# Other PSUM banks, and eleven fewer, for the zeros products at the head of a Nyströmformer attention and MLP kernel

## The chip, the core and the metric

The kernel runs on one core of one Trainium2 chip. The time is that of one execution on the device, in microseconds (us); lower is better. Before the change it is 262.47 us, the median of 3 runs (262.06 to 262.75).

## The reference

Inputs are q, k and v (batch 8, 8 heads, 576 positions, head size 64) and two weights. Per batch and head, with 32 landmarks, each the mean of 18 consecutive positions:

```python
q_lm = q.reshape(B, H, m, S // m, D).mean(axis=3)      # k_lm the same
A  = softmax(scale * q @ k_lm.T);  Bm = softmax(scale * q_lm @ k_lm.T);  C = softmax(scale * q_lm @ k.T)
Z  = Bm.T / (max column sum * max row sum + 1e-6)
for _ in range(6): Z = 2 * Z - Z @ Bm @ Z
x  = A @ Z @ C @ v                                     # heads side by side: 4608 rows of 512
out = square(maximum(x @ w_in, 0)) @ w_out             # w_in 512 x 2048, w_out 2048 x 512
```

The output is float32; on the chip the products are taken in bf16.

## The kernel before, in words

**What is computed where.** The work goes batch by batch. For one batch TensorE transposes q and k (L579) and sums them over each landmark's positions by products with a permutation matrix (L544, folded at L554); in the first two batches every one of these is a product on TensorE, with `perm` as the moving operand. From the sums come the landmark product Bm (L604 for batch 0, L607 for batch 1), on VectorE and ScalarE its softmax (L619 to L631) and transposed copy BTf (L633), and the start `st` of the iteration (L667, L669). Six products (L689 in batch 0) with an update each on VectorE (L704) give Z. Beside that run the scores of q against the landmarks (L873, then L884 to L912 on VectorE, POOL and ScalarE, up to the transposed matrix AT) and of the landmarks against k (L759; nmc, the negated maximum, L765; exponential L769; transposes L781; product with v L803). Z, that product and w_in are then multiplied into G (L853, L929), a 128 x 2 x 2048 matrix, so that the MLP's first layer is AT times G (L948), then relu and square (L965 to L975), then the second layer (L1020) and the stores.

**Overlap.** While the MLP of batch b runs, attention of batch b + 1 is worked in between. Only the head, batch 0, has nothing to run beside it.

**PSUM.** One tile `ps` holds the eight banks of 512 float32. Operations that need two neighbouring banks take the pairs 0-1 and 2-3; the others take single banks, 4 to 7. Which bank an operation takes is written in the order.

**The order.** `ORDER` (L40) is a list of integers, one operation each, in the order in which they are given to the engines. A positive code is 64 times the operation's number, plus 8 times the engine's (PE, ACT, DVE, POOL, SP), plus its bank. A negative code stands for zeros products:

```python
if code < 0:
    self.fill((-code) % 8, (-code) // 8)

def fill(bank, n):
    for _ in range(n):
        mm(ps[:, bank, 0:P], lhsT=zero[:], rhs=zero[:], start=True, stop=True)
```

So -479 is 59 products, 128 x 128 by 128 x 128, of a tile of zeros with itself, into bank 7. Nobody reads them. They keep TensorE at work where it would wait. They obey the same rules as other writers of a bank: the first of a set waits until what was in the bank has been read. Each engine works through its instructions strictly in order; semaphores between engines are set by a layer that tracks readers and writers of each tile region. `PACE` (below `ORDER`) adds waits by hand: an operation, mostly a load issued on POOL, then also waits for another operation.

**Loads.** q, k, v, w_in and w_out are loaded as float32 and cast to bf16 by DMAs issued on POOL; only the first half of k for batch 0 comes by SP in float32 and is cast by POOL and ScalarE (L304, L306). Stores go by SP.

**The head, in TensorE's order, with its sets of zeros products** (number and bank in the kernel before; the last column tells what stands behind and where it writes):

| set | products, bank | what follows it on TensorE |
|---|---|---|
| 1 | 59, bank 7 | first transposes of q (L579), bank 4; 9 sums over q (L544), bank 5 |
| 2 | 7, bank 7 | last transposes of k, bank 6 |
| 3 | 10, bank 6 | 18 sums over k (L544), bank 7; then 9 sums over q, 6 transposes, a fold, 6 transposes |
| 4 | 6, bank 4 | Bm (L604), bank 5 |
| 5 | 5, bank 4 | landmarks against k (L759), banks 0 and 1 |
| 6 | 1, bank 7 | first product of the iteration's start (L660), bank 5 |
| 7 | 9, bank 5 | first iteration (L689), bank 7 |
| 8 | 8, bank 4 | second iteration, bank 5 |
| 9 | 2, bank 7 | transposes of the exponentials (L781), bank 4 |
| 10 | 8, bank 7 | fourth iteration, bank 5 |
| 11 | 4, bank 7 | product with v (L803), banks 0 and 1 |
| 12 | 11, bank 7 | third part of G (L929), banks 0 and 1 |
| 13 | 5, bank 6 | fourth part of G, banks 2 and 3 |
| 14 to 16 | 1, 5 and 2, banks 7, 4, 4 | products of the MLP and of batch 1 |

Of the kernel before, what the change touches and what calls it, by code (L numbers as in the profile page):

```python
# [37 lines left out]
}  # L38

ORDER = [  # L40
    592, 32, 344, 280, 472, 720, -479, 2628, 2309, 160, 784, 408, 200, 88, -63, 2182, 2248, -86, 1607, 1664, 2696,
    1736, 2368, 2440, 2758, 1560, 1796, 1864, 2887, 2952, -52, 3013, 984, 2832, 6016, 3088, 3208, 3144, 1496, 2052,
    9734, 1927, 2120, 6096, 920, 2501, 2568, 1368, 1992, 6594, 1176, 3280, 3344, 856, 3408, 3536, 3464, -44, 4992,
    9476, 6672, 3600, 5072, 1048, 5128, 1112, -15, 3781, 3664, 3728, 3920, 3856, 9544, 4738, 4816, 4872, -77, 3975,
    4048, -68, 4101, 6160, -23, 5252, 4176, 5192, 6736, 4936, 1240, 4231, 4304, -71, 4357, 536, 4432, 5520, 5584,
    5320, 5383, 6232, 8772, 6280, 6352, 4485, 1432, 6808, 5448, -39, 5632, 4560, 4615, 9800, 6416, 9157, 6480, 5712,
    1304, 4688, 5890, 5760, 6856, 6928, 6992, 7064, 9606, 5968, 9216, 5832, 7168, 7240, 6544, 7362, 7312, 7432, 7120,
    8024, 7960, -95, 7552, 7696, 7496, 7624, 8455, 15170, 656, 15360, 8216, 8512, 15248, 15312, 9288, 9349, 9424,
    15432, 8584, 18328, 15554, 15744, 15632, 18456, 9680, 15496, 18392, 18264, 9031, 15816, 9096, 15896, 8645, -46,
    7746, 7824, 15936, 7880, 16008, 16088, 8848, 8902, 8976, -15, 16130, 16208, 8712, 8280, 15688, 16320, 16392, 9863,  # L50
    8088, 9936, 9992, 10056, -44, 13826, 13904, 16456, -20, 16512, 16584, 13250, 10128, 10192, 10256, 8152, 10312,
    10392, 10448, 10512, 16264, 13328, 10576, 13968, 22980, 23040, 16648, 23104, 16704, 16898, 16776, 16968, 8344,
# [1035 lines left out]
```

## Time and profile before

| | |
|---|---|
| median of 3 runs | 262.47 us |
| the profiled execution | 262.38 us |
| its span, first to last instruction | 260.7 us |
| mean granted TensorE clock | 0.998 |
| TensorE busy | 246.9 us, 95% |
| VectorE, ScalarE, POOL busy | 78%, 77%, 56% |
| moved by DMA | 28.60 MB |

All times inside the profile count from the start of the span; the execution's own time is 1.7 us longer. A timeline row gives start, duration, engine, line, operation, output and inputs, and, in brackets, how long the engine had stood idle and what ended that. Rows of one operation that follow each other are merged (x59). PE is TensorE's product, PEld its weight load. Products are pipelined, so that a merged row's duration ends later than the next row's start; the distance of two starts tells the pace. The row of a DMA issue gives the time that issuing took; the time from issue to landing stands in a view of its own.

### The profile page before, as it was taken

To read this page: it belongs to the slowest core of one execution; us is meant where nothing else is said; L and a number is where in the kernel's file an instruction comes from. 1 tells how busy PE (TensorE), PEld (TensorE's weight loads), DVE (VectorE), ACT (ScalarE), POOL (GpSimd) and SP (SyncE) were. 2 spreads that over 40 slices of the span, in tenths; PEclk is the share of its full clock that TensorE was granted. 3 is DMA by queue.
4 is the path that set the end of the run, shared out by engine and by line. 5 is a ranking of instruction groups with operands and counts; after the bars stand their busy time and mean duration, and the time that the engine had idled before them with its cause. 6 is when DMAs were issued, how large, how long until landed. Compare 5 with 4: busy or idle time off the path is not lost.

```text
span 260.7 us, 7783 instructions
## 1 busy us (share of the span) xinstructions
PE 246.9 (95%) x3012; PEld 147.2 (56%) x3051; DVE 202.1 (78%) x488; ACT 201.1 (77%) x417; POOL 146.4 (56%) x219
## 2 busy tenths in 40 slices
PE   8888889999999999999999999999999999999995
PEld 8866654545654555455645465555645556466552
DVE  0088789999998888979989889799998877934521
ACT  2586799997998898978997799866978877676410
POOL 7247675786777666765587456845464454531000
PEclk9999999999999999999999999999999999999999
DMA  6999999639901991097605981094503431013233
GB/s 161 209 178 167 189 208 208 112 51 164 213 14 24 195 214 51 2 153 176 119 4 87 212 174 31 22 191 105 97 11 48 103 73 43 0 44 70 62 93 112
DMA packets 20470, 28.60 MB, mean 110 GB/s; under 512 B 3280, under 2 KB 11728, under 8 KB 20432
## 3 DMA queue, kind: packets, MB, share of 16 engines
q0 software_dynamic: 13296, 18.06, 44.0%
q1 hardware_dynamic: 6848, 9.77, 13.0%
q8 instruction: 24, 0.39, 0.6%
q10 hardware_dynamic: 288, 0.26, 0.3%
q14 instruction: 14, 0.11, 0.1%
HBM read 36.70 MB, written 9.44 MB: 177 GB/s over the span
## 4 chain that ended last, share of the span: by engine, by line
PE 79%; DVE 8%; ACT 4%; issue 4%; POOL 4%; DVEq 0%; ACTq 0%
PE ps L1020 40%; PE ps L948 21%; PE ps L455 4%; PE ps L725 3%; PE ps L926 2%; POOL EA L901 2%; PE ps L544 2%; PE ps L781 2%; PE ps L803 2%; PE ps L694 1%; DVE SA L884 1%; ACT r L965 1%; POOL ks L512 1%; PE ps L579 1%; DVE nmc L765 1%
## 5 line engine op out<-in xcount | busy, mean ns | idle before, releaser
L1020 PE MATMUL ps<-w_out_bf,gs 128*128 128x512 bf16 (+1 forms) x553 | 139.1, 373 | 3.3 <-issue 2.2
L948 PE MATMUL ps<-AT,G 128*128 128x288 bf16 x512 | 79.0, 286 | 1.4 <-issue 0.8
L1020 PEld LDWEIGHTS <-gs 128*128 128x128 bf16 x592 | 53.5, 98 | 47.3 <-issue 8.1
L965 ACT ACTIVATE r<-ps 128x576 bf16<-128x576 f32 x108 | 68.1, 651 | 13.7 <-PE ps L948 11.6
L948 PEld LDWEIGHTS <-G 128*128 128x128 bf16 x512 | 48.7, 98 | 24.1 <-issue 1.1
L973 ACT ACTIVATE gs<-r 128x576 bf16<-128x576 bf16 x83 | 55.4, 682 | 4.1 <-DVE r L967 3.5
L975 POOL TENSOR_TENSOR gs<-r 128x576 bf16<-128x576 bf16 x22 | 25.2, 1151 | 18.3 <-DVE gs L975 9.4
L304 ACT CAST G<-ps 128x512 bf16<-128x512 f32 x47 | 24.8, 592 | 4.6 <-PE ps L926 3.1
L379 POOL DMA_DIRECT2D vraw<-in_v_dram x32 | 18.2, 570 | 16.9 <-DVE BTf L633 8.5
L304 ACT COPY o<-ps 128x512 f32<-128x512 f32 (+1 forms) x32 | 18.0, 569 | 11.6 <-PE ps L1020 11.6
L967 DVE TENSOR_SCALAR r<-ps 128x576 bf16<-128x576 f32 x20 | 15.1, 759 | 10.3 <-PE ps L948 7.9
L638 POOL TENSOR_TENSOR Pd<-st,ones_d 128x256 bf16<-128x256 bf16 x17 | 11.4, 671 | 12.2 <-DVE st L704 8.6
L746 ACT ACTIVATE EC<-ps,nmc 128x288 bf16<-128x288 f32 x24 | 11.7, 501 | 7.9 <-DVE nmc L739 6.3
L890 POOL TENSOR_TENSOR SA<-SA,mxA 128x576 f32<-128x576 f32 x12 | 13.9, 1161 | 6.8 <-DVE qs L512 3.8
L455 PE MATMUL ps<-zero 128*128 128x128 bf16 x143 | 13.4, 255 | 4.2 <-DVE zero L464 1.1
L901 POOL TENSOR_TENSOR EA<-EA,rA 128x576 bf16<-128x576 bf16 x13 | 15.0, 1158 | 2.5 <-DVE ks L512 1.0
L533 DVE STREAM_TRANSPOSE qT<-qraw 128x1152 bf16<-128x1152 bf16 x12 | 16.4, 1364 | 0.0
L533 DVE STREAM_TRANSPOSE kT<-kraw 128x1152 bf16<-128x1152 bf16 x12 | 16.1, 1348 | 0.0
L455 PEld LDWEIGHTS <-zero 128*128 128x128 bf16 x143 | 11.4, 118 | 5.5 <-issue 3.7
L704 DVE SCALAR_TENSOR_TENSOR st<-st,ps 128x128 bf16<-128x128 bf16 x40 | 11.1, 278 | 3.0 <-PE ps L689 1.1
L884 DVE STREAM_TRANSPOSE SA<-ps 128x576 f32<-128x576 f32 x16 | 12.0, 768 | 1.7 <-PE ps L725 1.1
L975 DVE TENSOR_TENSOR gs<-r 128x576 bf16<-128x576 bf16 x23 | 10.2, 450 | 3.5 <-ACT r L965 3.3
(146 smaller groups left out, 362.2 us busy)
## 6 DMA issues: line engine op xcount, KB each, us to landing
out_dram<-o SPq DMA_DIRECT2D x126, 64.0 KB, 3.2
qraw<-in_q_dram POOLq DMA_DIRECT2D x16, 288.0 KB, 5.6
vraw<-in_v_dram POOLq DMA_DIRECT2D x32, 144.0 KB, 5.6
kraw<-in_k_dram POOLq DMA_DIRECT2D x15, 288.0 KB, 6.5
w_in_bf<-in_moe_w_in_dram POOLq DMA_DIRECT2D x4, 512.0 KB, 7.8
w_out_bf<-in_moe_w_out_dram POOLq DMA_DIRECT2D x4, 512.0 KB, 9.3
out_dram<-o SPq DMA_DIRECT2D x3, 256.0 KB, 3.1
gs<-in_k_dram SPq DMA_DIRECT2D x2, 288.0 KB, 4.0
```

Of the source, the lines that this page charges most:

```text
L304: nc.scalar.copy(dst, src)
L379: nc.gpsimd.dma_start(vraws[z][p0:p0 + 32, :, :, :].rearrange("p g t d -> p g (t d)"), src[b].rearrange(order, i=2, t=SEG)[i, :, :, c * NJ ...
L455: mm(ps[:, bank, 0:P], lhsT=zero[:], rhs=zero[:], start=True, stop=True)
L533: add("hx", "DVE", lambda e, nm=nm, raw=raw, i=i: nc.vector.transpose(heads(nm)[:, i, :, :, :].rearrange("p t h r -> p (t h r)"), raw[:, i ...
L884: keep("a_t", add("a_t", "DVE", lambda e, sa=sa, i=i, part=part: nc.vector.transpose(part(SA).rearrange("p c j m -> p c (j m)") if quad el ...
L901: keep("a_mul", add("a_mul", "POOL DVE", lambda e, part=part, spread=spread: ENG[e].tensor_tensor(part(EA), part(EA), spread(part(rA)), AL ...
L948: mm(t[:, j, 0:HALF], lhsT=G[:, i, f * P:(f + 1) * P], rhs=AT[:, i, j * HALF:(j + 1) * HALF], start=(i == 0), stop=(i == 1))
L965: nc.scalar.activation(r.rearrange("p (j t) -> p j t", j=2), src, AF.Relu)
L967: nc.vector.tensor_scalar(out=r.rearrange("p (j t) -> p j t", j=2), in0=src, scalar1=0.0, scalar2=None, op0=ALU.max)
L973: nc.scalar.activation(dst, r[:], AF.Square)
L975: ENG[e].tensor_tensor(dst, r[:], r[:], ALU.mult)
L1020: mm(one(ok)[:, 0:hi - lo], lhsT=gs[:, f, x0:x0 + P], rhs=w_out_bf[:, f, lo:hi], start=(f == f0), stop=(f == f1 - 1))
```

## The change

Only `ORDER` changes, and in it only codes of zeros products. Everything else stands in the same order on every engine, and the operations keep their banks. Set 1 has 48 products instead of 59. Eleven sets write to another bank: sets 1, 2, 3, 4, 5, 10 and 11 to bank 0, set 6 to bank 5, set 7 to bank 7, set 8 to bank 5, set 9 to bank 4, set 13 to bank 2. So some now write the bank of the operation behind them, and some a bank of the pairs. The first product of a set then waits for the readers of its new bank.

```diff
 ORDER = [
-    592, 32, 344, 280, 472, 720, -479, 2628, 2309, 160, 784, 408, 200, 88, -63, 2182, 2248, -86, 1607, 1664, 2696,
-    1736, 2368, 2440, 2758, 1560, 1796, 1864, 2887, 2952, -52, 3013, 984, 2832, 6016, 3088, 3208, 3144, 1496, 2052,
-    9734, 1927, 2120, 6096, 920, 2501, 2568, 1368, 1992, 6594, 1176, 3280, 3344, 856, 3408, 3536, 3464, -44, 4992,
-    9476, 6672, 3600, 5072, 1048, 5128, 1112, -15, 3781, 3664, 3728, 3920, 3856, 9544, 4738, 4816, 4872, -77, 3975,
-    4048, -68, 4101, 6160, -23, 5252, 4176, 5192, 6736, 4936, 1240, 4231, 4304, -71, 4357, 536, 4432, 5520, 5584,
-    5320, 5383, 6232, 8772, 6280, 6352, 4485, 1432, 6808, 5448, -39, 5632, 4560, 4615, 9800, 6416, 9157, 6480, 5712,
+    592, 32, 344, 280, 472, 720, -384, 2628, 2309, 160, 784, 408, 200, 88, -56, 2182, 2248, -80, 1607, 1664, 2696,
+    1736, 2368, 2440, 2758, 1560, 1796, 1864, 2887, 2952, -48, 3013, 984, 2832, 6016, 3088, 3208, 3144, 1496, 2052,
+    9734, 1927, 2120, 6096, 920, 2501, 2568, 1368, 1992, 6594, 1176, 3280, 3344, 856, 3408, 3536, 3464, -40, 4992,
+    9476, 6672, 3600, 5072, 1048, 5128, 1112, -13, 3781, 3664, 3728, 3920, 3856, 9544, 4738, 4816, 4872, -79, 3975,
+    4048, -69, 4101, 6160, -20, 5252, 4176, 5192, 6736, 4936, 1240, 4231, 4304, -64, 4357, 536, 4432, 5520, 5584,
+    5320, 5383, 6232, 8772, 6280, 6352, 4485, 1432, 6808, 5448, -32, 5632, 4560, 4615, 9800, 6416, 9157, 6480, 5712,
...
-    15432, 8584, 18328, 15554, 15744, 15632, 18456, 9680, 15496, 18392, 18264, 9031, 15816, 9096, 15896, 8645, -46,
+    15432, 8584, 18328, 15554, 15744, 15632, 18456, 9680, 15496, 18392, 18264, 9031, 15816, 9096, 15896, 8645, -42,
```

## The prediction, made before the changed kernel had run

> **What bounds the kernel now.** I read the page's first part, then the busy times by stretch, then the timeline of the first 32 us, because every edit lies there. First the page: the span, each engine's busy time, and the group of zeros products.
>
> ```profile
> span 260.7 us, 7783 instructions
> ...
> PE 246.9 (95%) x3012; PEld 147.2 (56%) x3051; DVE 202.1 (78%) x488; ACT 201.1 (77%) x417; POOL 146.4 (56%) x219
> ...
> L455 PE MATMUL ps<-zero 128*128 128x128 bf16 x143 | 13.4, 255 | 4.2 <-DVE zero L464 1.1
> ```
>
> TensorE is the bound, and the 143 zeros products are only 13.4 us of its work; 4.2 us of its idle time end in front of one of them. Where that idle time lies, the stretches tell (length, busy time of PE, PEld, DVE, ACT, POOL, granted clock, DMA share, GB/s):
>
> ```profile
> 0.00:10.00 10.00, 8.05 (x92) 7.93 (x93) 0.61 (x4) 3.07 (x4) 6.60 (x16) 1.00 0.82 178
> 10.00:20.00 10.00, 8.83 (x190) 7.21 (x186) 6.43 (x19) 7.50 (x23) 3.58 (x8) 1.00 1.10 184
> 20.00:30.00 10.00, 8.69 (x221) 6.80 (x222) 8.35 (x21) 6.29 (x13) 6.70 (x8) 1.00 1.17 177
> 30.00:40.00 10.00, 8.86 (x101) 5.90 (x100) 8.16 (x19) 9.42 (x22) 7.84 (x12) 1.00 1.18 205
> ...
> 60.00:80.00 20.00, 19.63 (x257) 11.82 (x258) 19.56 (x50) 18.22 (x37) 14.37 (x20) 1.00 0.59 116
> ```
>
> From 60 us on TensorE is busy for 98% of the time, so what the head saves is kept to the end, if nothing but TensorE's order follows. In the first 40 us it is idle for 5.6 us, and there the sixteen DMA engines are full too (share above 1). So the head has two clocks: the chain of batch 0 through TensorE, ScalarE and VectorE, and the loads.
>
> **Step 1, eleven products fewer ahead of the first transposes.** The zeros products alone in the first stretch (length, PE busy and count, granted clock, DMA), then the timeline of the start, then the two loads' times to landing (last column):
>
> ```profile
> 1.06:6.80 5.74, 5.74 (x55) 1.00 0.83 194
> ```
>
> ```profile
> 1.06 6.22 PE L455 MATMUL ps<-zero 128*128 128x128 bf16 x59 [1.06 <-DVE zero L464]
> 1.34 0.74 POOL L374 DMA_DIRECT2D qraw<-in_q_dram  x1 [0.82 <-POOLq L1072]
> ...
> 2.07 0.55 POOL L374 DMA_DIRECT2D kraw<-in_k_dram  x1
> ...
> 6.37 0.67 ACT L304 CAST kraw<-gs 128x576 bf16<-128x576 f32 x1 [4.28 <-DMA gs<-in_k_dram]
> 7.12 0.50 PE L579 MATMUL ps<-perm,qraw 128*128 128x128 bf16 x6
> ...
> 7.96 0.55 PE L455 MATMUL ps<-zero 128*128 128x128 bf16 x7
> 8.35 0.50 PE L579 MATMUL ps<-perm,kraw 128*128 128x128 bf16 x6
> ...
> 8.88 0.80 ACT L304 COPY kT<-ps 128x768 bf16<-128x768 bf16 x1 [1.84 <-PE ps L579]
> 9.58 0.80 ACT L304 COPY qT<-ps 128x768 bf16<-128x768 bf16 x1
> 9.73 0.72 PE L455 MATMUL ps<-zero 128*128 128x128 bf16 x10 [0.89 <-ACT kT L304]
> ...
> 10.29 1.17 PE L544 MATMUL ps<-perm,kraw 128*128 128x128 bf16 x18
> ```
>
> ```profile
> qraw<-in_q_dram POOLq DMA_DIRECT2D x1, 288.0 KB, 4.7
> ...
> kraw<-in_k_dram POOLq DMA_DIRECT2D x1, 288.0 KB, 5.7
> ```
>
> A zeros product takes 5.74/55 = 0.104 us at the start; the fifteen q products take (7.96 - 7.12)/15 = 0.056 us each, and the ten zeros from 9.73 to 10.29 the same. TensorE starts at half speed, though the granted clock reads 1.00, and is fast from about 6.8 us. Eleven products fewer are 1.15 us at the slow pace, so the q transposes could start near 6.1 instead of 7.12. Their q lands at 1.34 + 4.7 = 6.04: no hindrance. But then 15 q products and 7 zeros follow, the first six or seven still slow (6.2 + 6 x 0.104 + 16 x 0.056 = 7.7), and the k transposes need k, landing at 2.07 + 5.7 = 7.8. With 0.15 us from landing to product they start at 7.95 instead of 8.35. **Gain 0.40**, not 1.15. In a run whose slow stretch ends earlier it is 0, with a later end up to 0.65.
>
> **Step 2, the ten zeros in front of the sums over k.** In the kernel before they go into bank 6 and wait until ScalarE has copied the k transposes out of it (8.88 + 0.80 = 9.68). The sums behind them need nothing of that copy: they go to bank 7, and the last of k that they read is cast at 6.37 + 0.67 = 7.04 (its other half has landed at 7.8). In bank 0 the zeros start behind the sixth transpose, 8.35 + 6 x 0.056 = 8.69 instead of 9.73: 1.05 us more, **1.45 in all**. ScalarE, next in the chain, has time: moved by 0.40 its second copy ends near 9.58 + 0.80 - 0.40 = 9.98, and the sums end near 10.0.
>
> **Step 3, six zeros in front of the first small product.**
>
> ```profile
> 12.24 0.50 PE L579 MATMUL ps<-perm,qraw 128*128 128x128 bf16 x6
> ...
> 12.44 0.37 ACT L304 CAST kdup<-ps 128x256 bf16<-128x256 f32 x1
> ...
> 12.87 0.49 PE L455 MATMUL ps<-zero 128*128 128x128 bf16 x6
> ...
> 13.29 0.23 PE L604 MATMUL ps<-kdup,qls 128*32 128x32 bf16 x8
> ```
>
> Zeros and product wait for the same cast (ends 12.81). Afterwards the zeros run while the cast does (12.58 to 12.91), and the product starts near 13.0 instead of 13.29: 0.29 more, **1.74**.
>
> **Step 4, the zeros ahead of the iterations.** The five and the one that come next lie beside a VectorE that is busy almost without a break (the row below, third engine); they are counted at nothing, and without that cover would be worth 0.1. Then the rows of the next two sets and of what waits for them:
>
> ```profile
> 14.80:18.50 3.70, 2.76 (x72) 1.96 (x69) 3.46 (x11) 2.87 (x7) 2.22 (x4) 1.00 1.19 186
> ```
>
> ```profile
> 17.64 0.21 DVE L667 TENSOR_TENSOR st<-BB,rc 128x64 bf16<-128x64 f32 x1
> ...
> 17.77 0.75 DVE L765 TENSOR_REDUCE nmc<-ps 128x1 f32<-128x576 f32 x1
> ...
> 18.36 0.24 PE L689 MATMUL ps<-st 32*32 32x64 bf16 x8
> ...
> 18.72 0.29 DVE L704 SCALAR_TENSOR_TENSOR st<-st,ps 128x128 bf16<-128x128 bf16 x1 [0.20 <-PE ps L689]
> ...
> 20.77 0.61 PE L455 MATMUL ps<-zero 128*128 128x128 bf16 x8 [0.62 <-DVE st L704]
> ...
> 21.61 0.29 DVE L704 SCALAR_TENSOR_TENSOR st<-st,ps 128x128 bf16<-128x128 bf16 x1 [0.88 <-PE ps L689]
> ...
> 23.09 0.70 ACT L893 ACTIVATE EA<-SA 128x576 bf16<-128x576 f32 x1
> ...
> 25.45 0.62 PE L929 MATMUL ps<-w_in_bf,WT 64*32 64x512 bf16 x16
> ```
>
> Nine zeros wait for the first half of st and hold the first iteration's products back to 18.36; without them in the way these start behind its second half (17.64 + 0.21), near 17.9, but its update stands behind nmc on VectorE (17.77 + 0.75 = 18.52), so 18.72 becomes 18.55: 0.17 more, **1.91**. Eight zeros at 20.77 wait for the update before, take 8 x 0.056 = 0.45 and with the change of tile 0.5, and hold the fourth iteration back by that, and the update at 21.61 with it: VectorE stands idle for it. The products with w_in at 25.45, though, wait for batch 0's other chain too (POOL's subtraction, EA at 23.09, its sum on VectorE), and of the 0.5 I count 0.2: **2.1**. The four zeros ahead of the products with v are counted at nothing: behind them VectorE works on that other chain.
>
> **Step 5, the loads.** Most loads after 8 us stand on POOL behind steps of this same chain, and so move with it:
>
> ```profile
> 15.30 1.11 POOL L379 DMA_DIRECT2D vraw<-in_v_dram  x2 [7.09 <-DVE BTf L633]
> ...
> 20.95 0.58 POOL L374 DMA_DIRECT2D kraw<-in_k_dram  x1
> ...
> 29.17 0.61 PEld L544 LDWEIGHTS <-kraw 128*128 128x128 bf16 x9 [0.71 <-DMA kraw<-in_k_dram]
> ...
> 31.86 0.44 PE L455 MATMUL ps<-zero 128*128 128x128 bf16 x5 [0.38 <-DVE qT L306]
> ```
>
> ```profile
> kraw<-in_k_dram POOLq DMA_DIRECT2D x1, 288.0 KB, 8.0
> ```
>
> POOL issues nothing for 7.09 us and then waits for BTf. From 10 to 30 us the queue moves 180 GB/s instead of the 205 of the next ten: 20 x 0.12 = 2.4 us of transfer are lost there, and that is the most that earlier issues can win back; the least is 0, if the full engines take the bytes no sooner. TensorE waits 0.5 us for k at 29.17, and the five zeros at 31.86 give 0.36 by their new bank. These two may add 0.9 to the 2.1; loads that follow only in part take from it. I take -0.2 for both together: a **gain of 1.9 us**.
>
> The profiled execution took 262.38 us, 1.7 more than its span, and stands 0.09 below the median of 262.47. 262.38 - 1.9 = 260.5.
>
> **The rivals.** *A, the loads don't follow.* If k of batch 1 lands at 20.95 + 8.0 = 28.95 as now, TensorE takes up at 29.17 as now, whatever the head saved, and only the 0.36 of 31.86 is left: 262.0. For it speaks the DMA share of 1.17; against it the 7.09 us and the dip in GB/s. If they follow by half, about 1.0 is left: 261.4.
>
> *B, the change doesn't do what it says at the start*: the slow stretch ends early, or k is late; then 0.4 goes, 260.9, inside the forecast's own range.
>
> *C, slower: the warm-up.* The 59 products also keep TensorE at work until it gets fast. If 48 and then transposes don't do, the slow pace goes on. Each product costs 0.048 us more; from 6.8 us up to the small product of step 3 there are 9 + 7 + 6 + 10 + 18 and some 28 more, about 80 of them, in the new order. It decides at 56 products, 2.7 us, that is, if the slow pace lasts from 6.8 to beyond 6.8 + 56 x 0.104 = 12.6 us: then the 1.9 are eaten and 0.8 is lost, 263.2 or more. Against it: q lands before the 48 end, so TensorE has no gap in that stretch. If it lasts only until the sums over k, the 9 + 7 + 6 + 10 = 32 products ahead of them cost 1.5 us (until 6.8 + 32 x 0.104 = 10.1 us) and leave 0.4 of the gain: 262.0.
>
> The Trainium skill bears on C: "TensorE: Matmul & The Clock Gate", Part 1, has half speed as the default, released after about 3.4 us of activity in a free-running window, and Part 4 says that transposes don't count as activity in the same way. The trace agrees with the half speed (0.104 against 0.056 us) and shows a release about 5.7 us after the first product; whether transposes count, it doesn't show. By that rule, with transposes in the window's last 0.7 us, the release could slip one window, to about 6.8 + 3.4 = 10.2 us: C's milder case.
>
> **How the numbers follow.** Forecast, 260.5 (own range 259.5 to 261.4): 0.58. A: 0.13 for half (261.4, still faster), 0.14 for nothing (262.0). C: 0.08 for the milder case, 0.07 for the slower one. About 0.3%, 0.8 us, is what a measurement of this kernel can tell from no change. Faster 0.58 + 0.13 = 0.71; same 0.14 + 0.08 = 0.22; slower 0.07. The range leaves out C's slower case and a gain of 3 us: 259.5 to 262.3.
>
> **What would show it.** After the change: the k transposes near 7.9; the sums over k near 8.8 and no ScalarE wait ahead of zeros; the small product near 11.5; the first products with w_in near 23.3; the load of k at 29.17 landing near 27, and TensorE behind it without a longer wait. Wrong would be: zeros products still at 0.104 us after 7 us, a DMA wait at 29 us grown from 0.5 to over 2 us, or the w_in products waiting for their weights.

## The result, and the profile after

| | kernel before | changed kernel |
|---|---|---|
| median | 262.55 us (4 runs, 262.06 to 262.75) | 259.85 us (4 runs, 259.64 to 260.30) |
| the profiled execution, its span | 262.38 us, 260.7 us | 259.70 us, 258.0 us |

The ratio of the times is 0.9902 [0.9882, 0.9922]: faster by 2.70 us where 1.9 was forecast. A repeat beside the last experiments gave 260.86 (7 runs, 259.69 to 261.39) against 262.55 (23 runs), ratio 0.9925 [0.9894, 0.9955]: 1.7 us. The eleven executions of the two measurements fall in two groups, seven from 259.64 to 260.30 and four from 260.86 to 261.39, and the forecast of 260.5 lies between the groups. Ratios here leave out executions more than 1.5% above the fastest of the same kernel.

Of the changed kernel, the span from the page, and from the groups by line on TensorE that of the zeros products; behind the bar the busy time, the mean of one in ns, and the idle time in front of them:

```profile
span 258.0 us, 7801 instructions
```

```profile
L455 PE MATMUL ps<-zero 128*128 128x128 bf16 x132 | 11.6, 241 | 1.1 <-DVE zero L464 1.1
```

Of the 4.2 us that TensorE stood idle in front of zeros products, 1.1 is left, the wait for the tile of zeros at the very start. So 3.1 us of such waits went, and 2.7 us of time came back. (The list under "The change" names twelve sets with a new bank, though it calls them eleven.) The stretches, as shown of before (length, busy time of PE, PEld, DVE, ACT, POOL, granted clock, DMA share, GB/s):

```profile
0.00:10.00 10.00, 8.04 (x111) 7.71 (x112) 0.61 (x4) 3.64 (x5) 6.59 (x16) 1.00 0.83 178
10.00:20.00 10.00, 9.44 (x199) 7.04 (x196) 7.80 (x24) 8.52 (x24) 5.50 (x10) 1.00 1.19 206
20.00:30.00 10.00, 9.09 (x206) 7.03 (x205) 8.90 (x20) 7.14 (x15) 6.44 (x10) 1.00 1.22 201
```

From 10 to 30 us the loads move 206 and 201 GB/s in place of 184 and 177. That is 10 x 22 + 10 x 24 = 460 KB, or 2.2 us at 205 GB/s: nearly all of the 2.4 that the prediction called the most. VectorE is busy 16.70 us of these 20 in place of 14.78. Both clocks of the head have moved.

The timeline of TensorE in the changed kernel (start, duration, operation, how often, and the idle time before it with what ended it):

```profile
1.06 4.35 PE L455 MATMUL ps<-zero 128*128 128x128 bf16 x48 [1.06 <-DVE zero L464]
6.07 0.51 PE L579 MATMUL ps<-perm,qraw 128*128 128x128 bf16 x6 [0.66 <-DMA qraw<-in_q_dram]
...
7.71 0.51 PE L579 MATMUL ps<-perm,kraw 128*128 128x128 bf16 x6 [0.23 <-DMA kraw<-in_k_dram]
8.05 0.72 PE L455 MATMUL ps<-zero 128*128 128x128 bf16 x10
8.61 1.17 PE L544 MATMUL ps<-perm,kraw 128*128 128x128 bf16 x18
9.62 0.67 PE L544 MATMUL ps<-perm,qraw 128*128 128x128 bf16 x9
...
11.33 0.23 PE L604 MATMUL ps<-kdup,qls 128*32 128x32 bf16 x8
...
15.94 0.24 PE L689 MATMUL ps<-st 32*32 32x64 bf16 x8 [0.40 <-DVE st L667]
...
18.52 0.24 PE L689 MATMUL ps<-st 32*32 32x64 bf16 x8
...
20.21 0.73 PE L803 MATMUL ps<-vraw,ECT 64*32 64x64 bf16 x71 [0.17 <-DMA vraw<-in_v_dram]
...
22.09 0.22 PE L853 MATMUL ps<-zt,cvb 32*64 32x32 bf16 x8 [0.38 <-DVE zt L714]
...
23.18 0.63 PE L929 MATMUL ps<-w_in_bf,WT 64*32 64x512 bf16 x16
...
24.89 0.41 PE L929 MATMUL ps<-w_in_bf,WT 64*32 64x512 bf16 x8 [0.37 <-DMA w_in_bf<-in_moe_w_in_dram]
...
27.34 1.14 PE L948 MATMUL ps<-AT,G 128*128 128x288 bf16 x8
...
29.21 0.41 PE L929 MATMUL ps<-w_in_bf,WT 64*32 64x512 bf16 x8
...
34.14 0.81 PE L1020 MATMUL ps<-w_out_bf,gs 128*128 128x512 bf16 x3 [0.16 <-DMA w_out_bf<-in_moe_w_out_dram]
```

The same products from the fourth iteration on in the kernel before, as far as the prediction doesn't show them:

```profile
21.31 0.24 PE L689 MATMUL ps<-st 32*32 32x64 bf16 x8
...
24.35 0.22 PE L853 MATMUL ps<-zt,cvb 32*64 32x32 bf16 x8
...
26.73 0.45 PE L929 MATMUL ps<-w_in_bf,WT 64*32 64x512 bf16 x8
...
29.90 1.14 PE L948 MATMUL ps<-AT,G 128*128 128x288 bf16 x8
...
32.23 0.41 PE L929 MATMUL ps<-w_in_bf,WT 64*32 64x512 bf16 x8
...
36.92 0.82 PE L1020 MATMUL ps<-w_out_bf,gs 128*128 128x512 bf16 x2
```

The sums over k follow their ten zeros at 8.61 with no wait for ScalarE; the kernel before had them at 10.29. The distance to the same product of the kernel before is 0.64 us at the k transposes, 1.68 at the sums, 1.96 at L604, 2.42 at the first iteration, 2.79 at the fourth, 2.27 at the first products with w_in, 1.84 at the third part of G (24.89), 2.56 at 27.34, 3.02 at 29.21 and 2.78 at the first L1020. From 45 us to the end most products stand 2.67 to 2.69 us earlier, all of them 2.46 to 3.12.

POOL's issues in the changed kernel, and then, from a view of the DMAs issued from 18 to 19 us, the time from issue to landing of k for batch 1:

```profile
13.35 1.10 POOL L379 DMA_DIRECT2D vraw<-in_v_dram  x2 [5.06 <-DVE BTf L633]
...
18.99 0.58 POOL L374 DMA_DIRECT2D kraw<-in_k_dram  x1
```

```profile
kraw<-in_k_dram POOLq DMA_DIRECT2D x1, 288.0 KB, 7.3
```

v is issued at 13.35 in place of 15.30, and k lands at 18.99 + 7.3 = 26.3 in place of 28.95: it was issued 1.96 us earlier, and it also came 0.7 us sooner after its issue.

### The profile page after: what moved, and what is told of

Same layout as the page of the kernel before. It is cut to its first block, busy times and chain, and to the rows that moved or that the text cites. A ratio compares the mean times of both kernels' runs of the same rounds, so it can differ in the third digit from the quotient of the medians.

```text
span 258.0 us, 7801 instructions
## 1 busy us (share of the span) xinstructions
PE 249.7 (97%) x3040; PEld 145.3 (56%) x3040; DVE 202.6 (79%) x488; ACT 201.0 (78%) x417; POOL 146.0 (57%) x219
## 4 chain that ended last, share of the span: by engine, by line
PE 80%; DVE 7%; DMA 6%; ACT 2%; issue 2%; POOL 2%; DVEq 0%; ACTq 0%; POOLq 0%
PE ps L1020 44%; PE ps L948 23%; DMA w_in_bf<-in_moe_w_in_dram 3%; PE ps L725 3%; PE ps L926 3%; DMA kraw<-in_k_dram 2%; PE ps L803 2%; PE ps L781 2%; PE ps L694 1%; DVE SA L884 1%; PE ps L544 1%; POOL EA L901 1%; PE ps L579 1%; DVE nmc L765 1%; POOL ks L512 1%
## 5 line engine op out<-in xcount | busy, mean ns | idle before, releaser
L1020 PE MATMUL ps<-w_out_bf,gs 128*128 128x512 bf16 (+1 forms) x592 | 147.2, 374 | 0.2 <-DMA w_out_bf<-in_moe_w_out_dram 0.2
L1020 PEld LDWEIGHTS <-gs 128*128 128x128 bf16 x592 | 53.6, 98 | 47.5 <-issue 8.1
L975 DVE TENSOR_TENSOR gs<-r 128x576 bf16<-128x576 bf16 x23 | 10.2, 451 | 3.5 <-ACT r L965 3.3
L455 PE MATMUL ps<-zero 128*128 128x128 bf16 x132 | 11.6, 241 | 1.1 <-DVE zero L464 1.1
L306 DVE CAST G<-ps 128x512 bf16<-128x512 f32 x17 | 11.2, 680 | 1.6 <-PE ps L926 0.9
```

The costliest lines, as they stand in the source:

```text
L975: ENG[e].tensor_tensor(dst, r[:], r[:], ALU.mult)
L1020: mm(one(ok)[:, 0:hi - lo], lhsT=gs[:, f, x0:x0 + P], rhs=w_out_bf[:, f, lo:hi], start=(f == f0), stop=(f == f1 - 1))
```

## The experiments

**The theory after the result**: the head is held by two clocks, the chain of batch 0 and the loads. POOL issues v and w_in behind BTf, so what is saved ahead of BTf (sets 1 to 4) moves both clocks, and what is saved behind it (sets 7, 10, 13) moves only the chain and is mostly taken back by the loads. Then set 3 should be worth more than its 1.05 us, and the other sets less without it. The rivals: the eleven products fewer do it; the chain alone does it, set by set; earlier loads alone would do it; and fewer zeros would be better still. Each kernel below was timed against the kernel before, whose median was 262.52 to 262.55 us in each set of comparisons (23 runs each). "Gain" at a place is the distance between the starts of the same product in two traces, the kernel before and the experiment.

**1. The shortening alone.**

```diff
 ORDER = [
...
-    -479,
+    -391,
...
```

> Only set 1 shortened, 59 to 48, still in bank 7; all other sets as before. Chain theory: the k transposes wait for their load, so the gain over the kernel before is 0 to 0.4 us, depending on when the slow pace ends in the run. Rival 'every product left out is TensorE time': 11 x 0.104 = 1.15 us.

Measured: 262.06 us (12 runs), ratio 0.9988 [0.9967, 1.001]. Eleven products fewer alone can't be told from nothing. The timeline of TensorE in this kernel shows where it stops:

```profile
7.69 0.51 PE L579 MATMUL ps<-perm,kraw 128*128 128x128 bf16 x6 [0.25 <-DMA kraw<-in_k_dram]
9.09 0.72 PE L455 MATMUL ps<-zero 128*128 128x128 bf16 x10 [0.89 <-ACT kT L304]
```

The k transposes start as soon as k has landed, and the ten zeros behind them still wait 0.89 us for ScalarE's copy.

**2. The banks alone.** The changed kernel with 59 products in set 1:

```diff
 ORDER = [
...
-    -384,
+    -472,
...
```

> All new banks, but set 1 keeps 59 products. Chain theory: 2.3 to 2.7 us faster than before, that is at most 0.4 slower than the changed kernel. Rival 'every product counts': 1.5 us faster than before.

Measured: 259.88 us (6 runs, 259.64 to 260.18), ratio 0.9896 [0.9877, 0.9916]. Within the measurement that is the changed kernel: the new banks bring it without the shortening.

Why the eleven products don't show, two rows of zeros products alone tell, both of the stretch 4.06 to 6.80 us (length, PE busy and count, granted clock, DMA). First the kernel before with sets 7 and 10 changed (experiment 5), then that of experiment 1:

```profile
4.06:6.80 2.74, 2.74 (x29) 1.00 1.09 256
```

```profile
4.06:6.80 2.74, 1.23 (x22) 1.00 1.08 257
```

In the 3 us ahead of this both ran 29. Here one goes on at 2.74/29 = 0.094 us, and the other at 1.23/22 = 0.056 us (the counts take in products cut by the edges, so that the true distances are somewhat longer). Their sets 1 begin alike, and the fast pace begins at 7.04 in the one execution and at 4.00 in the other. With 59 products it also began at 6.88 (kernel before), 6.70 (experiment 11), 4.77 (experiment 2) and 3.87 (experiment 3). This comes from execution to execution, not from the edit, and with k landing at 7.7 to 7.8 an early end leaves nothing for the shortening to win. Where the pace is slow for longer it does win: the kernel before, fast from 6.88, has its k transposes at 8.35, and experiment 10, with 48 products and fast from 6.44, at 7.67. How often an execution starts late isn't shown: the fast pace came after 6 us in three of the five traces with 59 products and in two of the eight with 48.

**3. Set 3 alone**, in the kernel before:

```diff
 ORDER = [
...
-    -86,
+    -80,
...
```

> Only set 3 (ten zeros ahead of the sums over k) moves from bank 6 to bank 0. Chain theory: 1.05 us faster than before, all of it kept to the end. Rival 'the loads decide': under 0.4, because the k of batch 1 at 29 us doesn't come earlier.

Measured: 260.75 us (6 runs), ratio 0.9925 [0.9904, 0.9946]: 1.8 us by one changed code. The timeline:

```profile
8.47 1.17 PE L544 MATMUL ps<-perm,kraw 128*128 128x128 bf16 x18
```

```profile
27.00 0.66 PE L544 MATMUL ps<-perm,kraw 128*128 128x128 bf16 x9
```

In this execution 0.79 was there at the k transposes already (an early fast pace), and the set adds 1.03, as worked out. That 1.82 stands unchanged down to 28 us. Then it grows to 2.29: k of batch 1 has landed in time, and the wait of 0.5 at 29.17 is gone. At the end 2.39 is left. Nothing is taken back; something is added. But the early start has a share in that: the trace of experiment 1, with no bank changed, starts nearly alike (7.69), its lead of 0.64 grows to 1.32 at the same place, and 1.07 is left at 45 us. Against experiment 1 set 3 is worth 1.3 us, by the traces and by the medians; against the kernel before, which has the same set 1, it is 1.8.

**4. Everything but set 3**:

```diff
 ORDER = [
...
-    -80,
+    -86,
...
```

> The changed kernel with set 3 put back to bank 6. Chain theory: loses 1.05 us of the 2.7, so 1.65 faster than before. If another wait stands close behind it (the gains overlap), it loses less than that.

Measured: 261.94 us (12 runs), ratio 0.9979 [0.9959, 1.0]: 0.6 us, much less than expected. Three of the twelve executions (262.33, 262.82 and 263.40) had a mean granted clock of 0.993; the median of the other nine is 261.52, 1.0 us below the kernel before, and still less than expected. Its timeline:

```profile
31.03 0.41 PE L929 MATMUL ps<-w_in_bf,WT 64*32 64x512 bf16 x8 [0.76 <-DMA w_in_bf<-in_moe_w_in_dram]
...
36.14 0.81 PE L1020 MATMUL ps<-w_out_bf,gs 128*128 128x512 bf16 x3 [0.36 <-DMA w_out_bf<-in_moe_w_out_dram]
```

The gain is 0.30 at the k transposes, 0.57 at L604 and 1.41 at the fourth iteration. Of that 0.89 is left at L853, behind the other chain of batch 0, and it is 1.57 where the wait for k is gone. Then the fourth part of G waits 0.76 us for w_in and the first L1020 0.36 for w_out; there 0.79 is left, at 45 us 0.68. So the loads gave 0.7 us and took 0.9 back, which fits the theory. The changed kernel's lead grew by 0.41 over the same way (2.27 to 2.68); here it shrank by 0.21.

**5. Sets 7 and 10 alone**, in the kernel before:

```diff
 ORDER = [
...
-    -77,
+    -79,
...
-    -71,
+    -64,
...
```

> Only sets 7 and 10 (ahead of the first and the fourth iteration) get their new banks. 'Chain alone' (each wait taken off the chain is kept): 0.4 to 0.6 us faster than before. 'Two clocks' (the loads of v and w_in are issued behind BTf, ahead of these sets, so they don't come earlier, and what these sets save is waited for again at w_in, k and w_out): under 0.2.

Measured: 262.33 us (11 runs), ratio 0.9988 [0.9978, 0.9997]: 0.2 us. In the trace 0.75 us are gained at the fourth iteration (20.56 in place of 21.31), 0.23 are left at the products with v, and 0.37 from 45 us on. The zeros ahead of the products with v, in their old bank, wait for ScalarE:

```profile
22.32 0.38 PE L455 MATMUL ps<-zero 128*128 128x128 bf16 x4 [0.69 <-ACT ECT L304]
```

Here the gain is lost to other work of batch 0, before any load takes part.

**6. Everything but sets 7 and 10**:

```diff
 ORDER = [
...
-    -79,
+    -77,
...
-    -64,
+    -71,
...
```

> The changed kernel with sets 7 and 10 put back. 'Chain alone': loses 0.4 to 0.6 of the 2.7 us, near 260.3. 'Two clocks': loses under 0.2, near 260.0.

Measured: 260.42 us (6 runs, 259.63 to 261.47), ratio 0.9919 [0.9896, 0.9942]. The interval overlaps that of the changed kernel in both measurements: what these sets add with the others in place can't be read from it.

**7. Set 1 taken out whole.**

```diff
 ORDER = [
...
-    -384,
...
```

> The changed kernel without set 1 (no zeros products ahead of the first transposes of q). If the products bring the fast pace on: TensorE starts work at 6.0 us at the slow pace and keeps it for some 3 to 6 us, 30 to 60 products at 0.05 us each, 1.3 to 3 us slower than the changed kernel, 261 to 263. If the pace has nothing to do with them: no change, 259.9.

Measured: 262.32 to 266.74 us (12 runs, median 265.26), ratio 1.0065 [1.0032, 1.0099]: slower than the kernel before. The nine executions that the ratio keeps have a median of 264.32, 3.5 us above the changed kernel's 260.86 of experiment 12. Without the zeros at the start TensorE's slow pace meets the chain itself. The timeline of an execution of 266.33, then two stretches (columns as above):

```profile
10.41 2.12 PE L544 MATMUL ps<-perm,kraw 128*128 128x128 bf16 x18
12.33 0.71 PE L544 MATMUL ps<-perm,qraw 128*128 128x128 bf16 x9
...
14.08 0.23 PE L604 MATMUL ps<-kdup,qls 128*32 128x32 bf16 x8
...
27.09 0.24 PE L853 MATMUL ps<-zt,cvb 32*64 32x32 bf16 x3 [2.04 <-issue]
```

```profile
22.50:26.06 3.56, 1.90 (x98) 1.38 (x95) 3.44 (x10) 1.77 (x4) 1.96 (x3) 1.00 1.13 174
26.06:32.88 6.82, 5.79 (x63) 4.08 (x63) 2.65 (x5) 2.65 (x6) 2.50 (x3) 0.50 1.21 194
```

The eighteen sums take (12.33 - 10.41)/18 = 0.107 us each where the changed kernel has (9.62 - 8.61)/18 = 0.056, and the fast pace begins only at 12.4 us. The small product L604 starts 2.75 us behind the changed kernel's (14.08 against 11.33). Later the granted clock falls to 0.50 for 6.82 us, 1.0 us into a stretch of 2.04 us in which TensorE waited for nothing that the profile shows. The seven executions from 265.21 us up, this one among them, had a mean granted clock of 0.986 or 0.987; the two quickest, 262.32 and 262.95, had 0.998 and 1.00. So the fall comes in many executions, not in all, and adds to what the start costs.

**8. The zeros products of the head taken out, but not set 1** (nor set 12): sets 2 to 11 and 13 gone.

```diff
 ORDER = [
...
-    -56,
-    -80,
-    -48,
-    -40,
-    -13,
-    -79,
-    -69,
-    -20,
-    -64,
-    -32,
-    -42,
...
```

> The changed kernel without sets 2 to 11 and 13: TensorE stands idle where they ran. 'Chain alone': they lie beside waits, so 259.7 to 260.1. If the idle time costs the fast pace (TensorE falls back to the slow one for a stretch in some executions): up to 1.7 us slower in those, a mean granted clock of 0.993, and a wide spread.

Measured: 260.38 us (6 runs, 259.90 to 260.89), ratio 0.9909 [0.9882, 0.9935]: no difference from the changed kernel that can be told. Beneath it two things work against each other. The head is 0.43 us further ahead at L604 (10.90 against 11.33). But first the rows of this kernel, then the one of the changed kernel for the same stretch:

```profile
12.83:16.25 3.42, 1.50 (x50) 0.94 (x46) 3.22 (x12) 2.54 (x8) 2.36 (x4) 1.00 1.18 208
16.25:23.07 6.82, 6.13 (x155) 4.84 (x156) 6.03 (x18) 4.69 (x12) 5.05 (x9) 0.50 1.23 206
```

```profile
12.83:16.25 3.42, 3.00 (x75) 2.03 (x73) 3.18 (x11) 2.74 (x7) 1.92 (x4) 1.00 1.17 205
```

TensorE is busy 1.50 us of 3.42 in place of 3.00, and for the next 6.82 us the granted clock is 0.50. The mean granted clock of all six executions is 0.985 to 0.993, so it fell in each of them. The zeros of the head cost some of its time and hold the clock; the gain against the kernel before falls from 3.14 at the fourth iteration to 1.68 at the third part of G, and is 2.68 from 45 us on, as in the changed kernel. At 121 us it drops to 2.0, where a product of a later batch waits for POOL:

```profile
121.04 0.23 PE L694 MATMUL ps<-st,Pd 128*128 128x64 bf16 x2 [0.49 <-POOL Pd L638]
```

**9. The changed kernel with earlier loads.** The waits by hand of the loads of v and of w_in's first two parts (operations 13, 16, 17 and 19) are removed; buffers and everything else stay.

```diff
 PACE = {
...
-    8: 75, 13: 52, 16: 55, 17: 55, 19: 60, 20: 101, 22: 105, 97: 96, 106: 67, 110: 109, 124: 114, 125: 102, 126: 253,
+    8: 75, 20: 101, 22: 105, 97: 96, 106: 67, 110: 109, 124: 114, 125: 102, 126: 253,
...
```

> The changed kernel without the four waits by hand that hold two loads of v and two of w_in behind steps of batch 0's chain. 'Two clocks': the waits for w_in at 24.5 us and for w_out at 34 us go, 0.2 to 0.5 us faster than the changed kernel, near 259.5. 'Chain alone': no change, 259.85.

Measured: 260.09 us (4 runs, 259.81 to 260.86), ratio 0.9899 [0.9884, 0.9914]: nothing on top of the changed kernel. Its timeline:

```profile
25.22 0.41 PE L929 MATMUL ps<-w_in_bf,WT 64*32 64x512 bf16 x8 [0.87 <-DMA w_in_bf<-in_moe_w_in_dram]
```

w_in was issued at 11.09 in place of 14.44 and 16.19, and yet the third part of G waits 0.87 us for it, more than the 0.37 of the changed kernel. At 206 GB/s from 10 to 20 us the changed kernel leaves next to nothing for earlier issues to win. No kernel tried here is measurably faster than the changed one.

This execution took 260.86 us, but not because of its head: at 45 us its gain is 2.68, that of the changed kernel. It loses 0.8 us at 121 us, where the same product as in experiment 8 waits, and here POOL had waited for a load of k:

```profile
117.30 1.55 POOL L512 TENSOR_TENSOR khalf<-kraw 128x576 bf16<-128x576 bf16 x1 [1.92 <-DMA kraw<-in_k_dram]
```

```profile
121.24 0.23 PE L694 MATMUL ps<-st,Pd 128*128 128x64 bf16 x2 [0.60 <-POOL Pd L638]
```

**10. Everything but set 3, with earlier loads**: experiment 4 with the edit of experiment 9.

> All new banks but set 3's, and without the same four waits. With the waits this kernel gained 0.6 us only. 'Two clocks': 1.3 to 1.7 us faster than before, since the loads no longer hold it. 'Chain alone': still 0.6.

Measured: 261.78 us (12 runs, 260.57 to 262.67, and one of 629 us that stands outside everything else), ratio 0.997 [0.9954, 0.9987]. Against experiment 4 that is no difference that the medians can tell, and the expectation missed. The profiled execution, at 260.57 the fastest, had its first L1020 at 34.38 and a gain of 2.44 us at 45 us, so the mechanism can work; why the other executions don't show it is open.

**11. The kernel before with earlier loads**: the edit of experiment 9 alone.

> The kernel before without the four waits by hand that hold two loads of v and two of w_in behind batch 0's chain; all zeros as before. 'Two clocks': the load of k at 29 us lands 1 us or more sooner and the idle time of 0.5 us there goes, 0.3 to 0.6 us faster than before. 'Chain alone': no change.

Measured: 262.56 us (12 runs), ratio 0.9992 [0.9975, 1.001]: nothing. The timeline:

```profile
36.79 0.81 PE L1020 MATMUL ps<-w_out_bf,gs 128*128 128x512 bf16 x3 [0.17 <-DMA w_out_bf<-in_moe_w_out_dram]
```

In this execution k of batch 0 landed late, and the k transposes start 0.39 us behind the kernel before's (8.74). k of batch 1 lands at 26.3 in place of 29.0, the wait for it goes and 0.37 is gained at 28.8 us. But w_out is issued behind the chain of batch 0 as before (26.84; before 26.53), the first L1020 starts only 0.13 us earlier than in the kernel before, and 0.03 is left from 45 us on. By the medians, earlier loads without an earlier chain are worth nothing; the trace, with its late start, can't exclude some tenths.

**12. The changed kernel once more**, no edit.

> The changed kernel once more, for the spread of its executions. Forecast's rival C (48 products don't always carry TensorE to the fast pace): some executions 1.5 us or more above the rest. Otherwise all within about 0.7 us, median 259.7 to 260.1.

Measured: 260.86 us (7 runs), ratio 0.9925 [0.9894, 0.9955], as told with the result. Its profiled execution took 260.00 us:

```profile
35.03 0.81 PE L1020 MATMUL ps<-w_out_bf,gs 128*128 128x512 bf16 x3 [1.12 <-DMA w_out_bf<-in_moe_w_out_dram]
```

The first L1020 starts 0.9 us later than in the first trace, and still the end lost only 0.3 (260.00 against 259.70). So a wait for w_out there need not cost its length. What makes the four slower executions isn't shown, since none of them was profiled; the loss at 121 us in experiment 9 is of a similar size.

## Why the prediction came out as it did

The direction, the place and the mechanism held: zeros products had waited for a reader of their bank with the chain behind them, and from other banks they don't. The gain forecast was 1.9 us; measured were 2.70 and, in the repeat, 1.7, so that the forecast stands between two measurements of the same kernel. By its steps, in the first trace, each as the gain that the step adds:

| step | forecast | in the trace |
|---|---|---|
| 1, set 1, at the k transposes | 0.40 | 0.64 |
| 2, set 3, at the sums over k | 1.05 | 1.04 |
| 3, set 4, at L604 | 0.29 | 0.28 |
| 4, sets 5 and 6 | 0 | 0.01, at the first product of the iteration's start |
| 4, sets 7 and 10, left at the w_in products | 0.17 + 0.2 | 0.30 |
| 5, loads, wait for k, set 13 | -0.2 | +0.41, from 2.27 to 2.68 |

- **Step 1** reached its bound for another reason. The forecast put k's landing at 7.8 and, without a row for it, 0.15 more to the product; k landed at 7.66 and the product followed after 0.05. But this execution was fast from 4.2 us, and then the shortening wins nothing, as the prediction said of "a run whose slow stretch ends earlier": the 0.64 is the difference between an execution with a late fast pace and one with an early one. With a late pace the shortening wins what was worked out (8.35 against 7.67, in experiment 2). By the medians of experiments 1 and 2 it can't be told from nothing.
- **Steps 2 and 3** came out to 0.01 us (step 2's own figures, 9.73 and 8.69, give 1.04). They were read from one row each, the end of the reader that the zeros waited for and the pace of the zeros.
- **Step 4** is right in its sum. The fourth iteration gained another 0.51 where 0.5 was worked out, and all of that was lost again up to L853: the products with v waited for their load (20.21), which the prediction had not counted, and L853 for VectorE (22.09). Experiment 5 shows a loss of the same size ahead of the products with v.
- **Step 5 is the term that was mis-sized**: -0.2 was taken, +0.41 came. The prediction knew that the loads move with the chain. It counted 0.9 for the wait for k and set 13, and took off 1.1 for loads that follow only in part, a size for which it had no row. In the trace the lead falls from 2.27 to 1.84 at the third part of G, which waits for w_in; rises to 2.56 behind the wait for k and to 3.02 by set 13; and falls to 2.78 at the first L1020 and 2.68 at 45 us. So about 1.2 came and 0.8 was taken back. The loads followed nearly in full, because set 3 lies ahead of BTf: 1.95 us of the chain are also 1.95 us of POOL's issues (15.30 to 13.35). Set 3 alone brings 1.8 us in place of its 1.05, or 1.3 against experiment 1; the others without it bring 0.6 to 1.0 in place of 1.65. That the place ahead of BTf decides is in part argued: experiment 1 shows that an early lead without new banks removes the wait for k too, and experiment 10, which should have freed the loads, missed.

**Rival A**, that the loads don't follow, fell for the whole change: k landed 2.6 us earlier. Waits of 0.17 us for v, 0.37 for w_in and 0.16 for w_out are new on TensorE. The wait for w_in was one of the prediction's signs of being wrong; it showed, but cost only 0.4 us. For the change without set 3 A holds in part: 0.9 of 1.57 us went back. **Rival B** came true in part: in the profiled execution the slow stretch ended early and the shortening won nothing, but the banks brought the time all the same. **Rival C**, the warm-up, didn't come. The changed kernel was fast from about 4.2 us, and another execution with 48 products, in experiment 10, from 6.4 with the k transposes at 7.67. Experiment 7 shows that its mechanism is real once there are no zeros at the start.

The prediction took it that what the head saves is kept to the end. In the changed kernel's trace it is (2.68 at 45 us, 2.7 in the time); in experiments 8 and 9 0.7 to 0.8 us of it went at 121 us.

For C the prediction weighed the Trainium skill, "TensorE: Matmul & The Clock Gate", Part 1 and Part 4. Part 1 also says that the window runs freely, so that the number of slow products changes from run to run. These traces agree: with 59 products the fast pace began at 3.87, 4.77, 6.70, 6.88 and 7.04 us. The slip to 10.2 us, which that rule would have allowed with 48 products, showed in no trace of them.

## What to carry to other kernels

Work that only keeps an engine awake still obeys the rules of the buffer that it writes. Look at what ended the idle time in front of it, and give it a buffer that nobody is reading, or one whose readers the operation behind it must await anyway. Where a stretch is held by a chain and by loads that are issued behind steps of that chain, price a saving by where it lies: ahead of such a step it moves both and was worth its full size or more here; behind it much was lost again, to the loads or to other work of the same batch. And look past the head: time saved early can meet a load further on that had not been in the way.

## What the runs showed of the hardware that was not expected

- TensorE's slow start ended between 3.87 and 7.04 us in executions whose start is the same, and the granted clock in the rows of that stretch reads 1.00 throughout (the two rows in experiment 2). The pace has to be read from counts or from distances of starts.
- The granted clock fell to 0.50 without a long gap. In experiment 8 TensorE's longest idle time between 6 and 24 us, weight loads aside, is the one in this row, and the clock fell after 3.42 us of which 1.50 were busy:

```profile
15.51 0.24 PE L689 MATMUL ps<-st 32*32 32x64 bf16 x8 [1.01 <-DVE st L667]
```

  In experiment 7 it fell after 1.90 of 3.56 us, 1.0 us into a gap of 2.04. In the kernel before it stayed with 2.76 of 3.70 (14.80 to 18.50 us, shown in the prediction), but in experiment 12 also with 1.81 of 3.41, no larger a share than in experiment 7:

```profile
31.63:35.04 3.41, 1.81 (x36) 1.20 (x29) 2.96 (x9) 3.27 (x11) 2.16 (x3) 1.00 1.19 202
```

  So where the limit lies, and whether the share over 3.4 us is all that counts, isn't shown. Each time the clock stayed down for 6.82 us. The Trainium skill, "TensorE: Matmul & The Clock Gate", "Why this matters for your kernels", asks for no idle gaps over about 3 us; here the clock fell behind 3.4 us with a busy share of 44% and no gap over 1.01 us, and the measurement decides.
